# Settling an instruction order by a rule about VectorE and GpSimd sharing SBUF, and dividing GpSimd's work anew by it

## The chip, the cores and the metric

One core of one Trainium2 chip. The metric is the device time of one execution in microseconds (us), the median of several executions.

Words used below: TensorE (PE), VectorE (DVE), ScalarE (ACT) and GpSimd (POOL) are the engines, with the short names that the profile gives them. In this kernel SBUF holds the tiles and PSUM the products of TensorE, bank by bank; a bank has to be read out before TensorE can fill it anew. A semaphore wait holds an operation back until another one has ended. A table load is ScalarE's ACT_TABLE_LOAD. Operations go by the names of the graph: b2, pr, pz, phi, norm, min.

## The reference, cut to what matters

Two blocks alternate twice over a 2048 x 512 input: linear attention with 32 heads of 16, and an MLP with 1792 hidden units. Each block normalises its input, and each adds its result to the residual.

```python
def _A_ref(x, wqkv, wo):
    qkv = ...                                   # x @ wqkv, split into q, k, v of 32 heads
    phi = lambda t: jnp.where(t > 0, t + 1, jnp.exp(t)) + 1e-6
    pq, pk = phi(q), phi(k)
    kv = jnp.einsum("bhsd,bhse->bhde", pk, v)
    num = jnp.einsum("bhqd,bhde->bhqe", pq, kv)
    den = jnp.einsum("bhqd,bhd->bhq", pq, z)[..., None] + 1e-6    # z: pk summed over the sequence
    return ... @ wo                             # num / den

x = x + _A_ref(_layernorm(x), A_wqkv, A_wo)
x = x + _B_ref(_layernorm(x), B_w1, B_b1, B_w2, B_b2)    # h = gelu(y @ w1 + b1); h @ w2 + b2
# ... and both once more
```

## The kernel before

The kernel first builds a graph of about 1500 operations. A list scheduler then settles each engine's order before anything is emitted: it holds a duration for every operation, searched priorities (`SHIFT`) and searched choices of engine (`WAY`). The emitted program has only these fixed lists and the semaphore waits that the graph needs. So the durations decide the order, but they do not run on the chip. This is where the order is settled (cut):

```python
            o.start = at
            dur = o.dur
            if o.fast and pool_busy > at:          # fast: held up by a large GpSimd operation
                dur += min(pool_busy - at, 600.0)
            if e == "pool" and o.sem is None and o.dur > 300.0:
                pool_busy = at + o.dur
            free[e] = at + dur
```

`fast=True` marks an operation that the list is to lengthen while a large GpSimd operation runs. It stands at the norm (one tensor source), at `min` (one source) and at the phi addition (two). The following do not have it, though on VectorE they read two tensors from SBUF:

```python
# pr: pq * 1/den, on VectorE or GpSimd by WAY      (in the profile: t<-t,lr, and t<-t,rr by token)
G.op("pool" if on_pool else "dve",
     lambda e, kt=kt, r=r: e.tensor_tensor(yTa(pq)[:, kt, :], yTa(pq)[:, kt, :], lr[:, r.slot, :], op=ALU.mult),
     1150 if on_pool else 600, ..., name=f"pr{tag}", lat=40)
# pz: pq * z, the same way                          (lr<-t,zrow)
# b2: the bias of the MLP into the residual, always GpSimd   (xsb<-xsb,b2b)
G.op("pool", lambda e: e.tensor_tensor(xsb[:, st, :], xsb[:, st, :], b2b[:], op=ALU.add), 1120,
     reads=[("x", st), "b2b"], writes=[("x", st)], prio=prio + 8, name=f"b2{L}_{st}")
```

The statistics of each norm go from VectorE (stats, mean and variance) to GpSimd (veps, rstd, nmr), then to VectorE or ScalarE (the norm itself), then through a transpose to TensorE. So GpSimd stands in the path of every norm.

Of the kernel before, what the change touches and what calls it, by code (L numbers as in the profile page):

```python
# [8 lines left out]
ALU = mybir.AluOpType  # L9

P = 128
# [99 lines left out]
class Scheduler:  # L111
# [13 lines left out]
    def run(self):  # L125
# [13 lines left out]
        pool_busy = 0.0  # L139
# [3 lines left out]
        while left:  # L143
            best = None
            for e in ENGINES:
# [3 lines left out]
                for o in released[e]:  # L149
                    at = max(o.ready, t0)  # L150
                    pr = o.prio
                    if o.table is not None and table is not None and o.table != table:
                        at = max(o.ready, t0 + TABLE_LOAD)
                        pr += self.table_penalty
                    ok = True
                    for t in o.tiles:
                        if t.slot is None:
# [4 lines left out]
                            if s > at:  # L162
                                at = s
# [16 lines left out]
            at, _, o = best  # L180
            e = o.eng
# [6 lines left out]
            dur = o.dur  # L188
            if o.fast and pool_busy > at:
                dur += min(pool_busy - at, 600.0)  # L190
            if e == "pool" and o.sem is None and o.dur > 300.0:
                pool_busy = at + o.dur
# [95 lines left out]
def assign_waits(graph, order, sems, dma_sems):  # L288
# [10 lines left out]
    while len(done) < total:  # L299
# [45 lines left out]
    N_HALF=1, N_K=1, N_Q=2, P_Z0=0, N_PB=1, N_PT=8, P_DEN=-55.81, P_A2=-10.5, P_W1=43.82, P_W2=90, P_K=42.81,  # L345
    P_G=138.05, P_Q=240, STEP=5.25, A1_Q=120, A1_STEP=3.25, N_H=3, N_N=1, GAP=2.76, TABLE_PENALTY=31.31,
    WINDOW=117.66,
    SHIFT={
        "B00_0": -22.2, "B00_1": -0.2, "B00_2": 71.0, "B00_3": 40.1, "B01": 36.0, "B02": 266.9, "B03": 104.1,
        "B10_0": 11.3, "B10_1": -23.9, "B10_2": 15.2, "B10_3": 66.3, "B11": 57.4, "B12": -26.2, "B13": -49.9,  # L350
        "D01": -7.0, "D02": 34.8, "D03": 8.7, "D10": -44.8, "D12": 7.7, "D13": -12.6, "G00_0": -29.6,
        "G00_1": 165.3, "G00_2": 99.7, "G00_3": 4.0, "G01_0": -124.2, "G01_1": 15.9, "G01_2": -16.0,
        "G01_3": -0.5, "G02_0": 67.0, "G02_1": 1.3, "G02_2": 124.4, "G02_3": 43.1, "G03_0": 2.8,
        "G03_1": 96.6, "G03_2": -15.0, "G03_3": 216.2, "G10": -252.6, "G11": 20.6, "G12": 17.0, "G13": -6.3,
        "K00_0": -63.5, "K00_1": 6.5, "K00_2": -64.9, "K00_3": -14.1, "K01_0": -2.5, "K01_1": -88.2,
        "K01_2": -64.3, "K01_3": -3.0, "K02_0": -6.7, "K02_1": 24.4, "K02_2": 41.1, "K02_3": -21.2,
        "K03_0": 2.5, "K03_1": -139.0, "K03_2": -39.8, "K03_3": 84.5, "K10": 71.5, "K11": 19.5, "K12": 60.3,
        "K13": 34.6, "N00_0": -102.6, "N00_1": -111.2, "N00_2": -96.7, "N00_3": -27.9, "N01_0": -143.7,
        "N01_1": -5.9, "N01_2": -55.3, "N01_3": -35.8, "N02_0": 1.8, "N02_1": 23.8, "N02_2": -19.5,
        "N02_3": 0.2, "N03_0": 29.0, "N03_1": 62.2, "N03_2": -16.1, "N03_3": 87.9, "N10": 21.0, "N11": 6.4,  # L360
        "N12": 0.9, "N13": -260.4, "O00_0": -200.3, "O00_1": 0.3, "O00_2": 6.2, "O00_3": 64.7, "O01": -2.8,
        "O02": 13.9, "O03": 45.5, "O10_0": 8.7, "O10_1": -39.3, "O10_2": -7.0, "O10_3": 15.1, "O11": -24.7,
        "O12": 192.0, "O13": 10.0, "Q00": 15.6, "Q01": -44.0, "Q02": 35.0, "Q03": 37.5, "Q10": 4.8,
        "Q11": -55.4, "Q12": 168.1, "Q13": -30.1, "U00_0": -11.7, "U01": 7.9, "U02": -174.6, "U03": -163.4,
        "U10_0": 1.3, "U10_1": -164.6, "U11": 34.9, "U12": -1.5, "U13": 0.6, "V0": 41.4, "V1": -6.3,
        "W00": -4.2, "W01": 78.8, "W02": 2.9, "W03": -84.7, "W10": -58.8, "W11": 229.0, "W12": 109.5,
        "W13": 185.3, "Z00": 30.0, "Z01": -14.8, "Z02": -74.5, "Z03": 27.7, "Z10": -6.5, "Z11": 18.8,
        "Z12": 18.3, "Z13": -161.7, "b1": 97.2,
# [3 lines left out]
        "TA0_6": "pe", "TA0_7": "pe", "TB0_0": "pe", "TB0_1": "pe", "TB0_2": "pe", "TB0_3": "pe",  # L372
        "TB1_0": "pe", "TB1_1": "dma", "TB1_2": "dma", "TB1_3": "dma", "cpg0_0": "dve", "cpg0_1": "act",
        "cpg0_2": "dve", "cpg0_3": "act", "cpg1_0": "act", "cpg1_1": "act", "cpg1_2": "dve", "cpg1_3": "act",
        "cpm0_0": "act", "cpm0_1": "dve", "cpm0_2": "dve", "cpm0_3": "act", "cpm1_0": "dve", "cpm1_1": "act",
        "cpm1_2": "dve", "cpm1_3": "act", "den1_2": "tok", "den1_3": "tok", "normA0_0": "dve",
        "normA0_1": "dve", "normA0_10": "dve", "normA0_11": "dve", "normA0_12": "dve", "normA0_14": "dve",
        "normA0_15": "dve", "normA0_2": "dve", "normA0_3": "dve", "normA0_4": "dve", "normA0_5": "dve",
        "normA0_6": "dve", "normA0_7": "dve", "normA0_8": "dve", "normA0_9": "dve", "normA1_0": "act",
        "normA1_1": "dve", "normA1_10": "act", "normA1_11": "dve", "normA1_12": "dve", "normA1_14": "act",  # L380
        "normA1_2": "act", "normA1_3": "dve", "normA1_4": "act", "normA1_5": "dve", "normA1_6": "act",
        "normA1_7": "dve", "normA1_8": "dve", "normA1_9": "dve", "normB0_0": "act", "normB0_1": "dve",
        "normB0_10": "act", "normB0_11": "dve", "normB0_12": "act", "normB0_13": "act", "normB0_14": "act",
        "normB0_15": "act", "normB0_2": "act", "normB0_3": "dve", "normB0_4": "act", "normB0_5": "dve",
        "normB0_6": "act", "normB0_7": "dve", "normB0_8": "act", "normB0_9": "dve", "normB1_0": "dve",
        "normB1_1": "dve", "normB1_11": "dve", "normB1_12": "act", "normB1_14": "act", "normB1_15": "dve",
        "normB1_2": "act", "normB1_3": "dve", "normB1_4": "act", "normB1_5": "act", "normB1_6": "act",
        "normB1_7": "act", "normB1_8": "dve", "normB1_9": "dve", "phik1_0": "pool", "phik1_13": "pool",
        "phik1_15": "pool", "phik1_7": "pool", "phik1_8": "max", "phiq0_0_3": "pool", "phiq0_1_2": "pool",
        "phiq0_2_0": "pool", "phiq0_2_2": "pool", "phiq0_3_0": "pool", "phiq0_3_1": "pool",  # L390
        "phiq1_0_1": "pool", "phiq1_0_3": "pool", "phiq1_2_3": "pool", "pr0_0_2": "pool", "pr0_1_0": "pool",
        "pr0_2_2": "pool", "pr0_3_1": "pool", "pr0_3_3": "pool", "pr1_0_1": "pool", "pr1_0_2": "pool",
        "pr1_0_3": "pool", "pr1_1_0": "pool", "pr1_1_1": "pool", "pr1_1_2": "pool", "pr1_1_3": "pool",
        "pr1_2_2": "pool", "pr1_2_3": "pool", "pr1_3_2": "pool", "pz0_0_0": "dve", "pz0_0_1": "pool",
        "pz0_0_2": "dve", "pz0_0_3": "pool", "pz0_1_0": "pool", "pz0_1_1": "pool", "pz0_1_2": "dve",
        "pz0_1_3": "dve", "pz0_2_3": "dve", "pz0_3_0": "pool", "pz0_3_2": "pool", "pz1_0_0": "pool",
        "pz1_0_1": "pool", "pz1_0_2": "dve", "pz1_0_3": "pool", "pz1_1_0": "pool", "pz1_1_1": "dve",
        "pz1_1_2": "pool", "pz1_1_3": "dve", "pz1_2_0": "dve", "pz1_2_1": "pool", "pz1_2_2": "dve",
        "pz1_2_3": "dve", "pz1_3_1": "dve", "pz1_3_2": "pool", "pz1_3_3": "dve",
# [4 lines left out]
def build_kernel(nc, A_x, A_wqkv, A_wo, B_x, B_w1, B_b1, B_w2, B_b2, out, conf=None, report=False):  # L404
# [5 lines left out]
    with ExitStack() as es:  # L410
# [37 lines left out]
        dz = SB("dz", [P, D], BF16)  # L448
# [96 lines left out]
        def eng(name):  # L545

            return cf["WAY"].get(name)
# [221 lines left out]
        def attn_kv(L, prio):  # L769
# [15 lines left out]
            if any(by_token(L, c) for c in range(NC)):  # L785
                zr = Tile(psum, f"zr{L}", "t")
                G.op("dve", lambda e: e.tensor_tensor(dz[:].rearrange("p (k c) -> p k c", k=DT), idp[:].unsqueeze(1).broadcast_to([P, DT, P]),
                                                      zs[:].unsqueeze(2).broadcast_to([P, DT, P]), op=ALU.mult), 600,
                     reads=["zs", f"id{P}"], writes=["dz"], prio=prio + 8, name=f"dz{L}", lat=40)
                G.op("pe", lambda e: e.matmul(bank(zr), lhsT=onesm[:, 0:P], rhs=dz[:], start=True, stop=True), MM,  # L790
                     reads=["dz", "onesm"], writes=[f"zr{L}"], tiles=[zr], prio=prio + 8, name=f"ZR{L}", lat=MM_DRAIN)
                copy(zrow[:], zr, f"zr{L}", "zrow", True, prio + 8, f"z{L}")
# [8 lines left out]
        def attn_den(L, c, pq, prio):  # L801

            G.grp = f"D{L}{c}"
            if by_token(L, c):
                pt = Tile(T4, f"pt{L}_{c}")
                for k in range(4):
# [8 lines left out]
                    def heads(ap):  # L815
# [4 lines left out]
                         reads=[f"pq{tag}", "zrow"], writes=[f"l{tag}"], tiles=[r, pq], prio=p, name=f"pz{tag}", lat=60)  # L820
# [12 lines left out]
                         name=f"pr{tag}", lat=60)  # L833
# [3 lines left out]
            for kt in range(DT):  # L837
# [14 lines left out]
                     reads=[f"l{tag}", f"pq{tag}"], writes=[f"pq{tag}"], tiles=[r, pq], prio=p, name=f"pr{tag}", lat=40)  # L852
# [20 lines left out]
        def mlp_front(L, c, k, yT, prio, on_act):  # L873
# [5 lines left out]
            else:  # L879
                transpose(y, ykey, yT, k, f"yB{L}_{st}", prio, f"B{L}_{st}")  # L880
            G.op("pool", lambda e: e.tensor_tensor(xsb[:, st, :], xsb[:, st, :], b2b[:], op=ALU.add), 1120,  # L881
                 reads=[("x", st), "b2b"], writes=[("x", st)], prio=prio + 8, name=f"b2{L}_{st}")
# [246 lines left out]
```

## Time and profile before

| | before |
|---|---|
| device time, median of 6 | 339.33 us (338.82 to 339.63) |
| span of the profile | 337.9 us |
| PE / VectorE / ScalarE / GpSimd busy | 325.9 / 201.9 / 242.7 / 141.1 us |

Two lines of the page, busy time by engine and the chain of work that ended last:

```profile
PE 325.9 (96%) x1759; PEld 161.4 (48%) x1791; DVE 201.9 (60%) x433; ACT 242.7 (72%) x392; POOL 141.1 (42%) x228
...
PE 75%; DVE 10%; POOL 8%; ACT 3%; issue 2%; DMA 1%; POOLq 0%
```

TensorE is the limit. A quarter of the chain nevertheless runs over other engines: those are the stretches in which TensorE waited for something that began earlier. Next, what PE waited for in the kernel before (line, releaser, us in total, times, longest):

```profile
PE ps L541 <- DVE onesm L506: 1.5, 1, 1.5
PE ps L605 <- DVE yb L582: 1.4, 3, 0.6
PE ps L865 <- DVE gtb L737: 1.4, 1, 1.4
PE ps L895 <- DVE xsb L939: 0.9, 1, 0.9
PE ps L895 <- DMA t<-yb: 0.8, 1, 0.8
PE ps L865 <- DVE outb L943: 0.7, 1, 0.7
```

The first is the start. The others that matter lie at 63 us (the 0.6 of L605), 55, 82, 156 and 247 us, in the order of the lines. How one of them comes about can be read in the timeline before it. Its columns are start, duration, engine, line, operation, tiles, shapes, and in brackets the idle time ahead of it:

```profile
80.27 1.15 POOL L881 TENSOR_TENSOR xsb<-xsb,b2b 128x512 f32<-128x512 f32 x1
80.54 1.43 DVE L850 TENSOR_TENSOR t<-t,lr 128x512 bf16<-128x512 bf16 x1
...
81.90 0.17 DVE L559 BATCH_NORM_AGGREGATE mv<-stats 128x2 f32<-128x6 f32 x1
81.99 0.65 DVE L939 TENSOR_TENSOR xsb<-ps,xsb 128x512 f32<-128x512 f32 x1
...
82.70 0.28 PE L895 MATMUL ps<-t,w 128*128 128x256 bf16 x1 [0.90 <-DVE xsb L939]
```

The product pr takes 1.43 us at 80.54, because a GpSimd addition (b2) began 0.27 us before it. VectorE's list goes on in order behind it, and the residual addition that frees a PSUM bank for TensorE comes late. The gap at 55 us is made the same way, by a phi addition on GpSimd:

```profile
52.59 1.15 POOL L643 TENSOR_TENSOR t<-eb,rb 128x512 bf16<-128x512 bf16 x1
...
53.01 1.28 DVE L850 TENSOR_TENSOR t<-t,lr 128x512 bf16<-128x512 bf16 x1 [0.57 <-ACT lr L846]
...
54.22 1.27 DVE L737 TENSOR_SCALAR gtb<-ps 128x512 bf16<-128x512 f32 x2
...
54.95 0.39 PE L865 MATMUL ps<-gtb,t 128*128 128x512 bf16 x1 [1.42 <-DVE gtb L737]
```

The groups by shape, where the mean is the last number ahead of the second bar (ns):

```profile
L582 DVE TENSOR_SCALAR yb<-xsb,mv,rstd 128x512 bf16<-128x512 f32 x24 | 19.1, 797 | 15.5 <-POOL rstd L569 15.3
L643 DVE TENSOR_TENSOR t<-eb,rb 128x512 bf16<-128x512 bf16 x23 | 12.5, 546 | 0.9 <-ACT rb L637 0.7
L850 DVE TENSOR_TENSOR t<-t,lr 128x512 bf16<-128x512 bf16 x12 | 9.5, 795 | 6.0 <-ACT lr L846 6.0
L870 DVE TENSOR_TENSOR xsb<-ps,xsb 128x512 f32<-128x512 f32 x16 | 10.7, 677 | 16.1 <-PE ps L865 15.8
```

Without a GpSimd operation beside them the norm, the phi addition and pr take 0.55, 0.42 and 0.68 us (medians of those in the trace that no large GpSimd operation overlaps). What an operation takes above that I call stretch. The residual addition of L870, with one operand in PSUM, does not stretch (mean 677 ns). I add up the duration above the undisturbed median for every VectorE operation that is over 60 ns above it: 17.5 us in 27 operations, 7.8 us of it in 11 operations that read two tensors from SBUF.

A second sum of mine is used below: TensorE's "lost time", the spacing of matmul starts beyond the pace of the matmul in front (0.216 us for 512 columns). It is 5.0 us up to 22 us, 2.1 us between 48 and 58 us, and 5.4 us elsewhere. 2.1 us of the first are the opening warm-up matmuls, which run at half pace. These sums are good to about 0.2 us, since some matmul records are missing.

### The profile page before, as it was taken

How to read it: one execution, taken by the hardware profiler on the slowest of the kernel's cores; microseconds unless marked ns; L12 is line 12 of the kernel's file. 1: busy time of each engine (PE TensorE's matmuls, PEld its weight loads, DVE VectorE, ACT ScalarE, POOL GpSimd, SP SyncE). 2: the span in 40 equal slices, each digit the busy share in tenths (PEclk: the TensorE clock that was granted, in tenths of full speed). 3: DMA queues.
4: the chain of work that ended last, by engine and by line, in shares of the span. 5: the costliest groups of instructions: out<-in, count | busy, mean ns of one | idle time of the engine just before them, and what ended most of it. 6: DMA issues, size and time to landing. Idle time of an engine off the chain costs nothing.

```text
span 337.9 us, 4861 instructions
## 1 busy us (share of the span) xinstructions
PE 325.9 (96%) x1759; PEld 161.4 (48%) x1791; DVE 201.9 (60%) x433; ACT 242.7 (72%) x392; POOL 141.1 (42%) x228
## 2 busy tenths in 40 slices
PE   7899998998999999998999999999989999999997
PEld 3444443565644444443444444448634444444444
DVE  6999547987256293476514789598795296420122
ACT  2988699989999979961984399859967667428000
POOL 5744422788237242265003224678765084220000
PEclk9999999999999999999999999999999999999999
DMA  8722660011101020023100110001333022120011
GB/s 260 253 57 56 216 236 0 3 31 34 31 17 33 16 47 17 0 57 53 31 16 7 26 32 2 1 18 31 64 93 90 5 48 51 28 63 0 31 35 61
DMA packets 38980, 18.15 MB, mean 54 GB/s; under 512 B 32620, under 2 KB 37996, under 8 KB 38956
## 3 DMA queue, kind: packets, MB, share of 16 engines
q1 hardware_dynamic: 35388, 10.63, 14.4%
q0 software_dynamic: 1056, 4.72, 4.0%
q10 hardware_dynamic: 2512, 2.49, 2.3%
q8 instruction: 14, 0.23, 0.2%
q14 instruction: 10, 0.08, 0.1%
HBM read 8.00 MB, written 2.10 MB: 30 GB/s over the span
## 4 chain that ended last, share of the span: by engine, by line
PE 75%; DVE 10%; POOL 8%; ACT 3%; issue 2%; DMA 1%; POOLq 0%
PE ps L895 23%; PE ps L933 21%; PE ps L656 7%; PE ps L865 5%; PE ps L687 4%; PE ps L753 4%; PE ps L721 4%; DVE xsb L870 3%; POOL rstd L569 2%; POOL xsb L881 2%; DVE stats L557 2%; PE ps L674 2%; PE ps L541 1%; DVE yb L582 1%; POOL nmr L574 1%
## 5 line engine op out<-in xcount | busy, mean ns | idle before, releaser
L895 PE MATMUL ps<-t,w 128*128 128x512 bf16 (+1 forms) x552 | 100.2, 336 | 2.2 <-DVE xsb L939 0.9
L933 PE MATMUL ps<-w,gT 128*128 128x512 bf16 x424 | 97.3, 379 | 0.7 <-DVE xsb L870 0.2
L901 ACT ACTIVATE gT<-ps,b1c 128x512 bf16<-128x512 f32 (+1 forms) x140 | 79.5, 602 | 20.1 <-PE ps L895 19.8
L895 PEld LDWEIGHTS ps<-t,w 128*128 128x128 bf16 x560 | 54.3, 98 | 46.3 <-DVE xsb L939 1.4
L933 PEld LDWEIGHTS ps<-w,gT 128*128 128x128 bf16 x434 | 42.1, 98 | 50.6 <-DVE xsb L870 0.7
L626 ACT ACTIVATE eb<-ps 128x512 bf16<-128x512 f32 x64 | 38.8, 617 | 20.8 <-PE ps L656 15.3
L569 POOL TENSOR_TENSOR rstd<-veps,neghalf 128x1 f32<-128x1 f32 x64 | 38.1, 595 | 7.5 <-DVE veps L567 2.5
L881 POOL TENSOR_TENSOR xsb<-xsb,b2b 128x512 f32<-128x512 f32 x32 | 37.9, 1188 | 6.4 <-DVE yb L582 4.4
L1065 ACT ACT_TABLE_LOAD x31 | 39.8, 1283 | 0.5
L637 ACT ACTIVATE rb<-ps 128x512 bf16<-128x512 f32 x63 | 38.3, 618 | 0.0
L865 PE MATMUL ps<-gtb,t 128*128 128x512 bf16 x126 | 31.5, 380 | 2.2 <-DVE gtb L737 1.4
L639 DVE TENSOR_SCALAR eb<-eb 128x512 bf16<-128x512 bf16 x63 | 20.0, 327 | 22.5 <-ACT eb L626 22.1
L557 DVE BATCH_NORM_STATS2 stats<-xsb 128x6 f32<-128x512 f32 x48 | 32.9, 685 | 1.0
L656 PE MATMUL ps<-wqkv,t 128*128 128x512 bf16 x123 | 32.0, 380 | 0.7 <-ACT t L615 0.3
L577 ACT ACTIVATE yb<-xsb,nmr,rstd 128x512 bf16<-128x512 f32 x24 | 19.1, 812 | 17.6 <-POOL nmr L574 17.4
L567 POOL TENSOR_SCALAR veps<-mv 128x1 f32<-128x1 f32 x29 | 7.2, 248 | 52.1 <-DVE mv L559 51.9
L582 DVE TENSOR_SCALAR yb<-xsb,mv,rstd 128x512 bf16<-128x512 f32 x24 | 19.1, 797 | 15.5 <-POOL rstd L569 15.3
L943 DVE TENSOR_TENSOR outb<-ps,xsb 128x512 bf16<-128x512 f32 x15 | 10.2, 683 | 28.4 <-PE ps L933 24.6
L562 POOL TENSOR_SCALAR veps<-mv 128x1 f32<-128x1 f32 x32 | 7.3, 230 | 40.4 <-DVE mv L559 38.8
L687 PE MATMUL ps<-t,wqkv 128*128 128x512 bf16 x95 | 23.6, 379 | 0.3 <-ACT t L615 0.2
L870 DVE TENSOR_TENSOR xsb<-ps,xsb 128x512 f32<-128x512 f32 x16 | 10.7, 677 | 16.1 <-PE ps L865 15.8
L865 PEld LDWEIGHTS ps<-gtb,t 128*128 128x128 bf16 x128 | 12.2, 98 | 17.0 <-DVE gtb L737 3.0
(79 smaller groups left out, 349.9 us busy)
## 6 DMA issues: line engine op xcount, KB each, us to landing
w<-in_B_w_dram POOLq DMA_DIRECT2D x4, 896.0 KB, 8.8
out_dram<-outb SPq DMA_DIRECT2D x15, 128.0 KB, 1.7
t<-in_A_x_dram ACTq DMA_DIRECT2D x3, 512.0 KB, 8.3
t<-yb SPq DMA_TRANSPOSE x51, 2.4
wqkv<-in_A_wqkv_dram SPq DMA_DIRECT2D x1, 512.0 KB, 5.5
wqkv<-in_A_wqkv_dram ACTq DMA_DIRECT2D x1, 512.0 KB, 7.3
wqkv<-in_A_wqkv_dram POOLq DMA_DIRECT2D x1, 512.0 KB, 6.3
wo<-in_A_wo_dram POOLq DMA_DIRECT2D x1, 512.0 KB, 5.8
```

Of the source, the lines that this page charges most:

```text
L557: G.op("dve", lambda e: e.bn_stats(stats[:, s.slot, :], src()), 620, reads=src_keys, writes=[k + "s"], tiles=[s, *src_tiles], prio=prio, n ...
L569: G.op("pool", lambda e: e.tensor_tensor(rstd[:, s.slot:s.slot + 1], veps[:, s.slot:s.slot + 1], neghalf[:], op=ALU.pow), 570, reads=[k + ...
L626: G.op("act", lambda e: e.activation(eb[:, et.slot, :], bank(bt), ACT.Exp), 478, reads=[src_key], writes=[f"e{tag}"], tiles=[bt, et], prio ...
L637: G.op("act", lambda e: e.activation(rb[:, rt.slot, :], bank(bt), ACT.Relu), 478, reads=[src_key], writes=[f"r{tag}"], tiles=[bt, rt], pri ...
L656: ins = e.matmul(bank(b), lhsT=yTa(yT)[:, dt, k * P:(k + 1) * P], rhs=wqkv[:, dt, D:2 * D], start=(dt == 0), stop=(dt == DT - 1))
L687: ins = e.matmul(bank(b), lhsT=wqkv[:, dt, kt * P:(kt + 1) * P], rhs=yTa(yT)[:, dt, :], start=(dt == 0), stop=(dt == DT - 1))
L865: ins = e.matmul(bank(wb), lhsT=yTa(pq)[:, kt, k * P:(k + 1) * P], rhs=gtb[:, kt, :], start=(kt == 0), stop=(kt == DT - 1))
L881: G.op("pool", lambda e: e.tensor_tensor(xsb[:, st, :], xsb[:, st, :], b2b[:], op=ALU.add), 1120, reads=[("x", st), "b2b"], writes=[("x", ...
L895: ins = e.matmul(bank(b, n), lhsT=w1[:, dt, ft * P:(ft + 1) * P], rhs=yTa(yT)[:, dt, k0 * P:k1 * P], start=(dt == 0), stop=(dt == DT - 1))
L901: G.op("act", lambda e, ft=ft, b=b, k0=k0, k1=k1, n=n: e.activation(gT[:, g.slot, ft * 512 + k0 * P:ft * 512 + k1 * P], bank(b, n), ACT.Ge ...
L933: ins = e.matmul(bank(b), lhsT=gT[:, g.slot, ft * 512 + k * P:ft * 512 + (k + 1) * P], rhs=w2[:, ft, :], start=(ft == 0), stop=(ft == FT - 1))
L1065: e.preload_act_table_set(sets[table])
```

## The change

Its intent: let the scheduler know that a VectorE operation with two tensors in SBUF waits until a large GpSimd operation has ended, all of it, and that GpSimd waits in turn; then search priorities and division of work anew under that rule. The arithmetic does not change. The core of the diff:

```diff
             if o.fast and pool_busy > at:
-                dur += min(pool_busy - at, 600.0)
+                dur += pool_busy - at - 60.0
+            if o.fast:
+                dve_busy = at + dur
             if e == "pool" and o.sem is None and o.dur > 300.0:
-                pool_busy = at + o.dur
+                dur += max(0.0, min(dve_busy - at, 400.0))
+                pool_busy = at + dur
@@ dz, pz, pr: now fast where they run on VectorE
-                         name=f"pr{tag}", lat=60)
+                         name=f"pr{tag}", lat=60, fast=not on_pool)
@@ b2: VectorE or GpSimd by WAY
-            G.op("pool", lambda e: e.tensor_tensor(xsb[:, st, :], xsb[:, st, :], b2b[:], op=ALU.add), 1120,
+            on_pool = eng(f"b2{L}_{st}") != "dve"
+            G.op("pool" if on_pool else "dve", lambda e: e.tensor_tensor(xsb[:, st, :], xsb[:, st, :], b2b[:], op=ALU.add),
+                 1120 if on_pool else 600, ..., fast=not on_pool)
@@ CONF: all of SHIFT and WAY new (cut). By count: b2 on VectorE 0 -> 15 of 32; phi additions on GpSimd 13 -> 21;
   pr on GpSimd 15 -> 20; fused max forms of phi 1 -> 8; transposes on TensorE 13 -> 11
```

## The prediction

> **What bounds the kernel now.** TensorE: on the page PE is 96% busy at full granted clock, and the chain that ended last is 75% PE, 10% VectorE, 8% GpSimd. In the timeline four 512-column matmuls start every 0.86 us. Start spacings beyond that pace (my sum) are what TensorE loses: 1.2 us before its first matmul, about 3.3 in the first 20 us, about 6 in five later gaps, about 3 after the last matmul. The timeline and PE's waits show the five: 53-55 us (1.4 idle), 63 (0.6), 82 (0.9), 156 (0.8), 247-250 (0.9). So no reordering can gain more than about 9 us (2.8%); the matmul work stays, but for two fewer PE transposes (4 x 56 ns each).
>
> **The rule is real.** In the timeline VectorE's eb+rb takes 0.42 us alone, 1.37-1.41 when it starts just after a 1.15 us GpSimd operation; pq*lr 0.68 and 1.29-1.43; t*rr 0.68 and 1.20; t*zrow 0.69 and 1.64. With one operand in PSUM it stays at 0.68. That agrees with the Trainium skill, "SBUF — State Buffer", section "Who interferes with whom": a VectorE instruction with two SBUF inputs contends with a GpSimd instruction that reads SBUF. Single-source norms stretch too (0.55 to 1.37). All stretches sum to 17.5 us of VectorE's 202. Before, the list model knew only norms, mins and phi additions, capped at 0.6; the others were taken as undisturbed. Three gaps end on such unmodelled stretch: pq*lr at 53.0 (0.6 extra), pq*lr at 80.6 (0.75), t*rr at 245.7 and what follows (0.5 + 0.8). The gap at 63 ends on a stretched norm (0.8), that at 156 on three b2 additions in GpSimd's queue (1.15 each) and a 4.0 us transpose.
>
> **What the change moves** (counted from the assignments): 15 of 32 b2 additions GpSimd to VectorE (-17.3 us GpSimd, +10.3 VectorE); phi additions on GpSimd 13 to 21, pr 15 to 20, pz 3 to 4 (+16 GpSimd, about -8 VectorE); 6 more fused max forms (+4 VectorE, -4 ScalarE); 4 norms net to VectorE; three more layer-0 transposes on DMA, one fewer in layer 1. Sums: GpSimd near 140 us, VectorE 198-208, ScalarE 233-241. None binds on average; only the phases at 40-85, 140-157 and 225-250 us matter. There, b2 off GpSimd shortens the rstd chain that PE waits for.
>
> **On the critical path.** Unmodelled stretch is worth about 3 us of the gaps. I expect the new order to recover about 2.5 of the 6 in the middle, 0.4 from transposes, a few tenths at the start, with small new waits giving some back: about -3 us. Head and tail are not touched by the rule.
>
> **Prediction: 336.3 us, 8 in 10 within 333.3 to 339.4.** Chances: faster by over 2% 0.07; within 2% 0.90; slower by over 2% 0.03.
>
> **What would show it.** PE busy near 325.5 and 96-97%; PE's waits in the middle from about 5 us to 2-3, without stretched pq*lr or t*rr at their ends; VectorE stretch from 17.5 to under 12; 17 b2 additions on GpSimd; the first 20 us lose as much as now.
>
> **What would make it wrong.** The order fitting its own model: queued DMA transposes (4.0 us against 2.4 typical) with more on that path; GpSimd's rstd delayed in long chains (0.99 against 0.55); more table loads (31 of 1.28 us now, and their penalty is lowered). If the head's 3.3 us shrink as well, 333 is reached.

## The result, and the profile after

| | before | after |
|---|---|---|
| device time, median of 6 | 339.33 us | 336.95 us (335.97 to 337.21) |
| ratio | 1 | 0.9926 (95%: 0.9911 to 0.9941) |
| PE / VectorE / ScalarE / GpSimd busy | 325.9 / 201.9 / 242.7 / 141.1 us | 326.4 / 203.6 / 222.6 / 139.7 us |
| stretch of VectorE, all / two-source | 17.5 us in 27 / 7.8 us in 11 | 13.3 us in 20 / 2.9 us in 4 |
| lost time of TensorE: to 22 us / 48 to 58 us / elsewhere | 5.0 / 2.1 / 5.4 us | 4.6 / 2.2 / 3.3 us |

A ratio is the mean time of one kernel's runs over that of the other's of the same rounds, so it is not quite the ratio of the medians quoted. Executions over 1.5% slower than the fastest of the same kernel are left out of the means. The last matmul starts 2.5 us earlier (335.1 to 332.5 us into the span, by my reading of the traces). 8 transposing matmuls fewer at 0.056 us each are 0.45 us of that, which leaves about 2.1 us of less waiting; the three sums of the table fall by 2.4, within what they are good to. PE's busy time cannot be compared so closely: the page of before holds 1759 matmul records, and 1791 are in the profiles of e5, e6, e9 and e10, which do the same matmuls.

The page of the kernel after, the same two lines:

```profile
PE 326.4 (97%) x1783; PEld 161.1 (48%) x1783; DVE 203.6 (61%) x439; ACT 222.6 (66%) x368; POOL 139.7 (42%) x224
...
PE 90%; DVE 3%; DMA 3%; ACT 1%; POOL 1%; issue 1%; POOLq 0%
```

The chain is now 90% TensorE, against 75%. What PE waits for, after:

```profile
PE ps L557 <- DVE onesm L522: 1.5, 1, 1.5
PE ps L672 <- DMA t<-yb: 1.1, 2, 0.6
PE ps L883 <- DVE gtb L753: 1.0, 2, 0.7
PE ps L915 <- DMA t<-yb: 0.6, 1, 0.6
PE ps L621 <- DVE yb L598: 0.6, 1, 0.6
PE ps L813 <- DVE kvb L809: 0.6, 1, 0.6
PE ps L859 <- DVE t L659: 0.3, 1, 0.3
```

The waits at 63, 82, 156 and 247 us are gone. New and smaller ones are there for transposes (22, 196, 297 us), at 134 us and at 215 us. The output step after the first attention (53 to 55 us) still waits. There pr is no longer stretched, since GpSimd starts nothing until 56.80:

```profile
52.80 0.68 DVE L867 TENSOR_TENSOR t<-t,lr 128x512 bf16<-128x512 bf16 x1
...
53.60 1.28 DVE L753 TENSOR_SCALAR gtb<-ps 128x512 bf16<-128x512 f32 x2
...
54.94 0.61 PE L883 MATMUL ps<-gtb,t 128*128 128x512 bf16 x2 [0.75 <-DVE gtb L753]
...
56.80 1.16 POOL L867 TENSOR_TENSOR t<-t,lr 128x512 bf16<-128x512 bf16 x1 [4.63 <-ACT lr L863]
```

The same groups as before, and what is new about b2 (its two lines are the two engines):

```profile
L598 DVE TENSOR_SCALAR yb<-xsb,mv,rstd 128x512 bf16<-128x512 f32 x28 | 20.0, 718 | 8.4 <-POOL rstd L585 8.0
L659 DVE TENSOR_TENSOR t<-eb,rb 128x512 bf16<-128x512 bf16 x18 | 9.4, 529 | 0.3 <-ACT rb L653 0.2
L867 DVE TENSOR_TENSOR t<-t,lr 128x512 bf16<-128x512 bf16 x10 | 6.8, 682 | 2.3 <-ACT lr L863 2.3
L900 POOL TENSOR_TENSOR xsb<-xsb,b2b 128x512 f32<-128x512 f32 x17 | 20.2, 1194 | 6.5 <-DVE yb L598 4.3 <-ACT yb L593 1.9 <-DVE mv L575 0.4
L900 DVE TENSOR_TENSOR xsb<-xsb,b2b 128x512 f32<-128x512 f32 x15 | 10.3, 687 | 5.8 <-ACT yb L593 5.7
```

pr of the form t<-t,lr on VectorE now has a mean of 682 ns against 795: not one of ten is stretched. (One pr of the other form, t<-t,rr at 241.40 us, still is, by 0.95 us; no wait of TensorE ends on it.) The norms still stretch (718, against 0.55 us undisturbed), and one phi addition is stretched right at a TensorE gap, in spite of the rule:

```profile
133.95 1.16 POOL L867 TENSOR_TENSOR t<-t,lr 128x512 bf16<-128x512 bf16 x1
...
134.02 1.37 DVE L659 TENSOR_TENSOR t<-eb,rb 128x512 bf16<-128x512 bf16 x1
...
135.45 0.39 PE L859 MATMUL ps<-t,zb 128*128 128x512 bf16 x1 [0.34 <-DVE t L659]
```

### The profile page after: what moved, and what is told of

The parts are those of the page before. It is cut to its first block, busy times and chain, and to the rows that moved or that the text cites. A ratio compares the mean times of both kernels' runs of the same rounds, so it can differ in the third digit from the quotient of the medians.

```text
span 335.3 us, 4848 instructions
## 1 busy us (share of the span) xinstructions
PE 326.4 (97%) x1783; PEld 161.1 (48%) x1783; DVE 203.6 (61%) x439; ACT 222.6 (66%) x368; POOL 139.7 (42%) x224
## 4 chain that ended last, share of the span: by engine, by line
PE 90%; DVE 3%; DMA 3%; ACT 1%; POOL 1%; issue 1%; POOLq 0%
PE ps L915 29%; PE ps L953 25%; PE ps L883 8%; PE ps L672 8%; PE ps L703 5%; PE ps L769 4%; PE ps L737 4%; DMA t<-yb 3%; PE ps L690 2%; PE ps L557 1%; PE ps L859 1%; DVE gtb L753 1%; PE ps L940 1%; PE ps L718 1%; DVE yb L598 1%
## 5 line engine op out<-in xcount | busy, mean ns | idle before, releaser
L655 DVE TENSOR_SCALAR eb<-eb 128x512 bf16<-128x512 bf16 x56 | 18.8, 343 | 41.2 <-ACT eb L642 40.8
L585 POOL TENSOR_TENSOR rstd<-veps,neghalf 128x1 f32<-128x1 f32 x64 | 38.8, 606 | 7.3 <-DVE veps L583 2.3
L653 ACT ACTIVATE rb<-ps 128x512 bf16<-128x512 f32 x56 | 34.2, 618 | 0.0
L593 ACT ACTIVATE yb<-xsb,nmr,rstd 128x512 bf16<-128x512 f32 x20 | 16.2, 811 | 23.8 <-POOL nmr L590 23.0
L659 POOL TENSOR_TENSOR pkb<-eb,rb 128x512 bf16<-128x512 bf16 x11 | 12.8, 1169 | 35.9 <-ACT rb L653 18.3
L598 DVE TENSOR_SCALAR yb<-xsb,mv,rstd 128x512 bf16<-128x512 f32 x28 | 20.0, 718 | 8.4 <-POOL rstd L585 8.0
L867 POOL TENSOR_TENSOR t<-t,lr 128x512 bf16<-128x512 bf16 x14 | 16.3, 1162 | 20.6 <-ACT lr L863 20.6
L900 POOL TENSOR_TENSOR xsb<-xsb,b2b 128x512 f32<-128x512 f32 x17 | 20.2, 1194 | 6.5 <-DVE yb L598 4.3
L672 PEld LDWEIGHTS ps<-wqkv,t 128*128 128x128 bf16 x128 | 12.0, 98 | 16.4 <-ACT t L631 1.3
```

The source lines that it names most:

```text
L585: G.op("pool", lambda e: e.tensor_tensor(rstd[:, s.slot:s.slot + 1], veps[:, s.slot:s.slot + 1], neghalf[:], op=ALU.pow), 570, reads=[k + ...
L598: G.op("dve", lambda e: e.tensor_scalar(yb[:, y.slot, :], src(), mv[:, s.slot, 0:1], rstd[:, s.slot:s.slot + 1], op0=ALU.subtract, op1=ALU ...
L653: G.op("act", lambda e: e.activation(rb[:, rt.slot, :], bank(bt), ACT.Relu), 478, reads=[src_key], writes=[f"r{tag}"], tiles=[bt, rt], pri ...
L672: ins = e.matmul(bank(b), lhsT=yTa(yT)[:, dt, k * P:(k + 1) * P], rhs=wqkv[:, dt, D:2 * D], start=(dt == 0), stop=(dt == DT - 1))
```

## The experiments

Theory A: TensorE's gaps end on VectorE operations that were held up by GpSimd; the new order keeps GpSimd operations from starting just ahead of those, and that is the gain. Rival B: the gain is the new order as such (fewer transposes on TensorE, 21 table loads after the first instead of 31, 20 us less work on ScalarE). Rival C: the gain is that 15 b2 additions left GpSimd. Eleven kernels ran. "Before" beside each is the kernel before on the same chip.

| run | time, us | before, us | ratio (95%) |
|---|---|---|---|
| e1 before, GpSimd only writes | 336.78 | 339.01 | 0.9933 (0.9912 to 0.9954) |
| e2 after, GpSimd only writes | 336.01 | 339.01 | 0.9909 (0.9890 to 0.9929) |
| e3 before, b2 moved | 336.82 | 339.01 | 0.9934 (0.9914 to 0.9953) |
| e4 after, b2 moved back | 337.12 | 339.01 | 0.9941 (0.9920 to 0.9962) |
| e5 before, four waits (two-source) | 337.46 | 339.00 | 0.9961 (0.9942 to 0.9981) |
| e6 before, four waits (single-source) | 337.64 | 339.00 | 0.9961 (0.9946 to 0.9976) |
| e7 after, mended | 335.60 | 339.00 | 0.9903 (0.9886 to 0.9919) |
| e8 new rule, old settings | 358.25, one look | 339.00 | none |
| e9 before, all eight waits | 335.97 | 339.12 | 0.9906 (0.9887 to 0.9925) |
| e10 before, five waits elsewhere | 339.18 | 339.12 | 1.0001 (0.9975 to 1.0026) |
| e11 after, mended, matmuls forward | 335.08 | 339.12 | 0.9880 (0.9862 to 0.9897) |

### e1 and e2: the contention taken away, the order kept

Every large addition or product on GpSimd became two memsets that write SBUF and read nothing. The order of all engines is settled as in the parent kernel, and each stand-in waits for the one before. Their outputs are wrong, which doesn't matter for the times.

```diff
+        def fill(e, ap):
+            e.memset(ap, 1.0)               # 512 columns, the operation's own output
+            return e.memset(dump[:], 1.0)   # 800 columns, for the duration
-                 lambda e: e.tensor_tensor(dst(), eb[:, et.slot, :], rb[:, rt.slot, :], op=ALU.add),
+                 (lambda e: fill(e, dst())) if on_pool else (lambda e: e.tensor_tensor(...)),
@@ likewise for pz, pr and b2 where they run on GpSimd
```

> The kernel before in its own order, its large GpSimd additions and products replaced by memsets of about the same length (1.0 to 1.2 us), which write SBUF but read nothing; the result is wrong on purpose. Theory A (two-source VectorE operations that wait for a GpSimd operation end TensorE's gaps, and avoiding that is the gain): the two-source stretch falls from 7.8 us to under 1, the norms (single source) stay stretched, the gaps at 53, 82 and 247 us shrink by 0.5 us or more each, and the time falls by 1.5 to 2.5 us, to 336.9 to 337.9. Rival B (the gain is the new order and its fewer transposes, whatever the contention): the time falls by under 0.7 us, 338.6 or more.

> The same replacement in the kernel after (wrong result on purpose). Theory A: there is little two-source waiting left to remove (2.9 us of stretch, none at a large gap), so 0 to 0.6 us faster than the kernel after, 336.3 to 337.0, and its distance to the kernel before with the same replacement is under 1.2 us. Rival B: as much faster as the kernel before becomes, the distance stays 2 us or more.

From e1's groups by shape:

```profile
L551 POOL MEMSET dump<- 128x800 bf16 x63 | 48.9, 777 | 0.0
...
L550 POOL MEMSET xsb<- 128x512 f32 x32 | 17.0, 530 | 5.9 <-DVE yb L590 3.4 <-ACT yb L585 1.8
...
L590 DVE TENSOR_SCALAR yb<-xsb,mv,rstd 128x512 bf16<-128x512 f32 x24 | 18.6, 778 | 18.2 <-POOL rstd L577 17.9
...
L652 DVE TENSOR_TENSOR t<-eb,rb 128x512 bf16<-128x512 bf16 x23 | 9.4, 412 | 1.6 <-ACT rb L645 1.4
L862 DVE TENSOR_TENSOR t<-t,lr 128x512 bf16<-128x512 bf16 x12 | 8.2, 684 | 6.2 <-ACT lr L857 6.2
```

The stand-in is no shorter than what it replaces (0.53 + 0.78 us, 1.23 from start to end as the two overlap a little, against 1.15), so GpSimd was not relieved. (It no longer waits for VectorE either; in before, 5 of its 63 large operations are 0.12 to 0.45 us longer than 1.15, 1.4 us in all.) Two-source operations of VectorE now all run at their undisturbed time (412 and 684 ns), and their stretch is 0 us. The norms are stretched as before (778 against 797). The time fell by 2.2 us, as theory A said (336.78, where 336.9 to 337.9 was expected). By lost time, the gap at 55 us fell from 1.37 to 0.77, that at 82 from 1.06 to 0.58, that at 156 from 1.01 to 0.54, and the two at 247 to 250 us (0.85 and 0.35) are gone; that at 63 us, which a norm makes, stayed at 0.8. In the kernel after, the same replacement was worth 0.9 us by the medians (0.6 by the ratios), more than the 0 to 0.6 expected; it had been 2.4 us ahead of before, and with the contention gone from both it is 0.8 us ahead. So about two thirds of the change's gain is two-source waiting. The 0.8 us that are left are not clear of noise (the intervals of e1 and e2 overlap) and are not taken apart further; 0.45 us of them could be the fewer transposing matmuls.

### e3 and e4: the b2 division alone, in both orders

No order is settled anew here: the 15 additions change engine and take the place in the other engine's list that their start had. e4 does the reverse with the kernel after.

```diff
+MOVE = {'b20_0': 'dve', 'b20_1': 'dve', 'b20_3': 'dve', ...}     # the 15 that the change moved
         order = sch.run()
+        for o in G.ops:
+            if o.name in MOVE:
+                order[o.eng].remove(o)
+                o.eng = MOVE[o.name]
+                order[o.eng].append(o)
+                order[o.eng].sort(key=lambda q: q.start)
```

> The kernel before in its own order, with only the 15 b2 additions that the change gives to VectorE moved there, each at the place in VectorE's list that its start had. Theory C (the b2 division is the gain, it frees GpSimd's rstd chain and takes blockers away): 1.5 us or more faster than before, 336.5 to 337.8, and the gaps at 63, 82 and 247 us shrink. Theory A (the order as a whole): within 1 us of before either way, since VectorE's 10 us of more work falls in its busy phases too.

> The kernel after in its own order, with its 15 VectorE b2 additions given back to GpSimd at the same places. Theory C: 1.5 to 3 us slower, 338.5 or more. Theory A: slower only where a b2 now blocks a two-source operation, 0.3 to 1.5 us, 337.3 to 338.5; if the b2 division is only filler, within 0.4 us of 336.95.

e3 gave 2.2 us: theory C had it right, and what I had written for theory A (within 1 us) was wrong. The gaps at 63 and 82 us shrank to 0.15 and 0.26 and those at 247 to 250 us went; the one at 55 us, which a phi addition makes, stayed at 1.36, and the one at 156 us, which ends on a transpose, grew from 1.01 to 1.23. But e4 took the division back out of the kernel after and lost nothing that its interval can show: 0.9941 beside 0.9926 for the kernel after. So moving b2 is one way to take GpSimd operations out from in front of VectorE in the old order; in the new order it is not needed. e4 shows one thing more, in its norms and mins:

```profile
L600 DVE TENSOR_SCALAR yb<-xsb,mv,rstd 128x512 bf16<-128x512 f32 x28 | 23.4, 838 | 12.6 <-POOL rstd L587 12.2 <-PE ps L771 0.2
L657 DVE TENSOR_SCALAR eb<-eb 128x512 bf16<-128x512 bf16 x56 | 22.5, 408 | 39.6 <-ACT eb L644 39.3
```

These norms were at 718 in the kernel after. All stretch together is 21.1 us here, more than in the kernel before, and yet the time is 1.9 us better than before. The sum of stretch is no measure of the time.

### e5, e6, e9 and e10: only waits added to the kernel before

The sharpest test moves no work: a GpSimd operation gets one more dependency, on the VectorE operation that it had held up. Every kernel of this group computes the reference.

```diff
+YIELD = {'phiq0_2_0': 'pr0_1_1', 'b20_7': 'pr0_2_1', 'b21_4': 'phiq1_3_3', 'b21_5': 'pr1_3_3'}    # e5, two-source
+# e6: {'b20_0': 'normB0_1', 'b20_4': 'normB0_3', 'b20_6': 'normB0_7', 'b21_7': 'minq1_2_0'}      # single-source
+# e9: both.  e10: {'b20_8': 'phiq0_3_2', 'phik1_13': 'phik1_11', 'phik1_15': 'phiq1_1_3', 'b21_3': 'phiq1_3_0', 'b21_9': 'pz1_2_3'}
         order = sch.run()
+        named = {o.name: o for o in G.ops}
+        for late, first in YIELD.items():
+            named[late].deps[named[first]] = True
```

> The kernel before, nothing moved: four GpSimd operations (one phi addition at 52 us, b2 at 80, 241 and 245 us) get one more wait each, for the two-source VectorE operation that they stretched at the end of a TensorE gap. A wait is added, no work is taken away. Theory A: the four two-source stretches (0.6, 0.75, 1.0, 0.5 us) vanish, the gaps at 53, 82 and 247 us shrink by about 0.6, 0.6 and 0.8 us, the time falls by 1.2 to 2.0 us, to 337.1 to 337.9. Rival (GpSimd's own queue sets the gaps): later GpSimd operations cost as much, the time stays within 0.5 us of before.

> The same with four b2 additions (62, 68, 78, 248 us) that stretched a single-source VectorE operation (three norms by 0.8 us, one min by 0.9). The list of before already reckoned with those, up to 0.6 us. If only the unreckoned two-source part matters: under 0.6 us faster than before. If any stretch that ends in a gap counts the same: 0.8 to 1.5 us faster, with the gap at 63 us gone (0.6) and that at 82 us shorter.

> The eight added waits of the two runs before (four for two-source, four for single-source operations) together in the kernel before; nothing else. If the stretches at TensorE's gaps are what the change is worth: the two gains (1.5 and 1.4 us) overlap at 82 and 247 us, so 2.0 to 2.8 us in all, 336.2 to 337.0, as fast as the kernel after (336.95) within 0.6 us, without its new division of work. If the division is worth something of its own: at least 0.8 us slower than the kernel after.

> A control: the same kind of wait at five two-source stretches of before that end in no TensorE gap (phi additions at 121, 196, 201 and 232 us, t*zrow at 280 us), together 4.0 us of stretch, more than the 2.9 us of the four waits for two-source operations that gave 1.5 us. If where a stretch ends decides: within 0.5 us of before, though the two-source stretch falls to about 4 us. If the sum of stretch counts: 1.5 us or more faster.

The timeline of e5 at the place shown for before, 52 to 55 us:

```profile
53.00 0.69 DVE L852 TENSOR_TENSOR t<-t,lr 128x512 bf16<-128x512 bf16 x1 [0.57 <-ACT lr L848]
...
53.77 1.15 POOL L645 TENSOR_TENSOR t<-eb,rb 128x512 bf16<-128x512 bf16 x1 [1.14 <-DVE t L852]
...
54.35 0.99 PE L867 MATMUL ps<-gtb,t 128*128 128x512 bf16 x3 [0.61 <-DVE gtb L739]
```

pr takes 0.69 us in place of 1.28, GpSimd starts its addition 1.2 us later, and TensorE goes on 0.60 us earlier. The four waits of e5 gave 1.5 us by the medians, the four of e6 1.4 us, all eight 3.1 us: the kernel before with eight more waits is as fast as the kernel after (335.97 beside 336.95, ratios 0.9906 and 0.9926; the intervals overlap). I had expected the two effects to overlap, and they did not: e9 came out under the 336.2 to 337.0 that I gave.

The waits did not take the stretch away; for the most part they moved it. Summed as above, the two-source stretch is 6.7 us in e5 and 7.2 in e9, against 7.8 before, and all stretch 15.3 and 14.2, against 17.5. In e5 the fourth named operation (t*rr, now at 242.85 us) is still held up by 0.42 us, and the gaps at 247 to 250 us shrank by 0.4 us where I expected 0.8. In e9 a pr takes 1.66 us at 78.63, and no wait of TensorE ends on it. e6 also shows that a stretch of a single-source operation at a gap costs about as much, though the old list reckoned with it. And e9 keeps the old 31 table loads, the old division and the old transposes. So a gain of this size needs none of rival B's points. That they gave nothing in the kernel after is not shown; e1 and e2 leave them 0.8 us. What PE waits for in e9:

```profile
PE ps L543 <- DVE onesm L508: 1.5, 1, 1.5
PE ps L607 <- DVE yb L584: 0.8, 2, 0.6
PE ps L867 <- DVE gtb L739: 0.6, 1, 0.6
PE ps L897 <- DMA t<-yb: 0.2, 1, 0.2
```

The control e10 took 4.0 us of two-source stretch away at places that end in no gap (7.8 us down to 3.8), and the time did not move: 1.0001, with an interval of about 0.9 us to either side. Single-source operations took over some of it, so all stretch fell by 2.5 us (17.5 to 15.0): more than e5's 2.2, which gave 1.5 us. Where a stretch ends decides.

### e7 and e11: the same medicine for the kernel after

e7 gives pr at 134 us a wait for the phi addition, the phi addition at 193 us a wait for the norm, and moves the b2 addition at 291 us. e11 also takes three groups of matmuls forward in TensorE's list, into gaps that no contention made.

```diff
+YIELD = {'pr0_3_1': 'phiq0_3_3', 'phik1_12': 'normA1_15'}      # e7 and e11
+MOVE = {'b21_10': 'dve'}                                       # e7 and e11
+AHEAD = {'G0_4_0': 'K0_8', 'Q0_2_3': 'WO0_0_0', 'Q1_3_2': 'WO1_0_2'}   # e11: before that one in TensorE's list
```

> The kernel after with the same medicine at three of its own remaining gaps: pr at 134 us waits for the phi addition that it stretched by 0.95, the phi addition at 193 us waits for the norm that it stretched by 0.93, and the b2 addition at 291 us, ahead of an rstd in GpSimd's queue, goes to VectorE. Theory A: the gaps at 134 (0.5), 196 (0.7) and 297 us (0.8) shrink, 1.0 to 1.8 us faster than after, 335.1 to 336.0. If the new order has filled behind those gaps already, the time stays within 0.5 us of 336.95 and new waits turn up elsewhere.

> The mended kernel after (335.6) with three groups of matmuls taken forward in TensorE's list into the gaps that no contention made: a G group ahead of the K that waits for a transpose at 22 us (0.8), a Q group ahead of the first output matmul at 54 us (0.9), a Q group at 214 us (0.4). If these are plain ordering gaps: 1.4 to 2.1 us faster than 335.6, that is 333.5 to 334.3, the best of all. If the delayed consumers give it back: over 335.

e7 came out as expected, 1.35 us under the kernel after by the medians (0.8 by the ratios, and the intervals overlap; the two were not timed in the same call): the gaps at 134 and 196 us vanished, that at 297 us fell from 0.80 to 0.11 us of lost time. e11 is the best kernel, correct, at 335.08 us, but it gave 0.5 us by the medians (0.8 by the ratios) of the 1.4 to 2.1 that I expected. The gaps at 22 and 54 us are filled (0.8 and 0.9 us), but new ones of 0.44 us at 57, 0.5 us at 219 to 221 and 0.4 us more at 295 us came behind them. That is what I had written for delayed consumers that give it back (over 335); why the gaps came is not tested.

### e8: the rule without new settings

```diff
-CONF of after
+CONF of before        # SHIFT, WAY and all parameters; the scheduler's code is that of after
```

> The new rule in the list order with all settings (priorities and assignments) of before. If the rule is the gain by itself: 336.5 to 338. I expect the settings to be fitted to the old rule and the list to fall apart under the new one: slower than before, over 342 us, with PE waits of several us; then the rule works only together with settings searched anew under it.

358.25 us, in one look, with state unknown and a granted clock of 0.975, so not a fast run to be compared closely; but it took 19 us more, and 18 of them are lost time of TensorE (30.9 us in all, against 12.5). About 4 of the 18 are matmuls at half pace behind its two longest waits, where the granted clock was 0.64 (99 to 104 us) and 0.54 (237 to 244 us); most of the rest are waits. Rule and settings belong together: priorities that were searched under one set of durations did not carry over to another here. The reverse, the new settings under the old rule, could not be built, for the scheduler finds no operation that can start; so the four corners of rule and settings are not complete.

## Why the prediction was right, point by point

- **Time.** 336.3 us was predicted, 333.3 to 339.4; 336.95 was measured, 2.4 us less than before where 3 were expected, within 2% as given a chance of 0.90. That the number is so near is in part luck, as the sums below show.
- **What bounds.** Right: TensorE at 97%, at most about 9 us to be had. The best kernel is 4.0 us under before.
- **"Unmodelled stretch is worth about 3 us of the gaps."** Mechanism right, size close: e1, without any two-source waiting, is 2.2 us faster, and four waits at the places named and one more (e5) gave 1.5. But the prediction drew the line in the wrong place. Single-source stretch, which the old list did reckon with, was worth 1.4 us more (e6).
- **"2.5 of the 6 in the middle, 0.4 from transposes, a few tenths at the start."** By lost time, the middle (from 22 us on) fell from 7.5 to 5.5 us, so 2.0. It was made up of far more on both sides: the gaps at 63, 82, 156 and 247 us gave 4 us, and new ones at 134, 196, 215 and 297 us took 2.6. Fewer transposes are 0.45 us, the start is 0.4. The term that was mis-sized is "small new waits", and it was made good by a recovery that was larger than the 2.5 expected: two errors that nearly cancel.
- **"There, b2 off GpSimd shortens the rstd chain."** Half right: in the old order it is worth 2.2 us (e3), in the new order nothing that shows (e4).
- **"PE's waits in the middle from about 5 us to 2-3."** Right in direction, short in size: PE's waits later than 20 us into the span fell from 4.7 to 3.6 us. The 17 b2 additions on GpSimd came as said.
- **VectorE 198-208 us, GpSimd near 140.** Right: 203.6 and 139.7. **ScalarE 233-241** was wrong: 222.6, mostly because the table loads behind the first fell from 31 to 21 (12.9 us of the 20) where I feared more. It did not matter, as e9 with its 31 loads shows.
- **"VectorE stretch to under 12."** Wrong: 13.3 us. e4 and e10 show that this sum was a poor sign to choose.
- **"Without stretched pq*lr or t*rr at their ends."** Right to the letter, but a stretched phi addition makes the gap at 134 us.

## What to carry to other kernels

When two engines hold each other up, find the few held operations that the critical engine waits for, and let the blocker wait for them: eight added waits gave 3.1 us here, at least as much as a new search over the whole program, and left two-source stretch at 7.2 of 7.8 us, while taking 4.0 us of it away elsewhere gave nothing that shows. Do not judge a schedule by the sum of its stretch or by busy time. And an order that was searched under one set of durations may have to be searched again when a duration changes (e8, a single look).

## What the Trainium skill lacked or had wrong

- "SBUF — State Buffer", section "Who interferes with whom", says that a VectorE instruction with two SBUF inputs contends with a GpSimd instruction that reads SBUF and not with one that only writes. e1 agrees: no two-source operation was stretched beside memsets, where 11 were (7.8 us) beside additions. The same section has 2-port modes of VectorE contend with GpSimd in any case; the norms agree if they ran in such a mode, which no view of the profile names (mean 797 ns in before and 778 in e1, 0.55 us undisturbed).
- That section says that whichever instruction issues first keeps the shared ports for all its length and the other fully blocks, but no page says how much longer the record of a held VectorE instruction becomes for a given overlap. Here it is less than the overlap: pr at 80.54 us began 0.88 us before GpSimd's end and took 0.75 us more than undisturbed; a norm at 61.92 us began 1.09 us before it and took 0.82 more. In before the difference is 0.13 to 0.14 us for all 11 stretched two-source operations and 0.25 to 0.26 us for all 9 stretched norms. That this much of the operation runs under the wait is my reading of it, and not tested.
- No page has what such a stretch is worth to a kernel: 4.0 us of two-source stretch less gave 0.0 us (e10), and eight waits at TensorE's gaps, which took 0.6 us of it away, gave 3.1 us (e9).
